# Splitting a kv normalization between VectorE and ScalarE, and moving one weight cast to GpSimd

## The chip, the cores and the metric

The kernel runs on one core of one Trainium2 chip. The metric is the device time of one execution in microseconds (us). Executions were taken in rounds beside executions of the kernel before on the same chip. The granted clock, where it is given, is the share of full speed that the throttle left to the tensor engine (PE) over the whole execution.

## The reference

Linear attention (softmax of q over its last axis, softmax of k over the sequence, no square score matrix), then a two-layer network with a swish gate:

```python
q_s = softmax(q, axis=-1); k_s = softmax(k, axis=2)            # q, k, v: (8, 8, 576, 64)
kv  = np.einsum('bhsd,bhse->bhde', k_s, v)                      # 64 x 64 per batch and head
x   = np.einsum('bhsd,bhde->bhse', q_s, kv)                     # -> (4608, 512)
h   = x @ w_in                                                  # 512 -> 2048
out = (h / (1 + np.exp(-beta * h))) @ w_out                     # 2048 -> 512
```

## The kernel before

The work goes batch by batch; the argument is about the first batch only, before the tensor engine is in full swing. Heads are taken in four pairs, the two heads of a pair on partitions 0 to 63 and 64 to 127. For each pair: kv by 18 small matmuls with a column of sums beside it, its normalization into `kvp`, one matmul that makes x transposed, an eviction of x into `xT`, then the up-projection h. Names in profiles: `kv`, `kvp`, `x`, `xT`, `h`, `th` (tanh), `g`, `acc` (output).

```python
def kvz_norm(b, j, n=1):
    t = att_of.pop((b, j, n))                        # PSUM: 128 x 65, kv and its sum
    rk = work.tile([P, n, 1], F32, tag="rk", bufs=2, ...)
    nc.vector.reciprocal(rk[:], t[:, :, D : D + 1])
    for e in range(2):                               # upper half, lower half
        r = slice(e * D, (e + 1) * D)
        nc.vector.tensor_tensor(
            kvp[r, b, j : j + n, e * D : (e + 1) * D], t[r, :, 0:D], rk[r].to_broadcast((D, n, D)), ALU.mult
        )
...
def xpe(c, j, tag):                                  # x of one pair, in PSUM bank `tag`
    t = x_ps[c, j] = ps.tile([P, MAIN], F32, tag=bank(tag), bufs=1, ...)
    nc.tensor.matmul(t[:], kvp[:, c, j, :], qsT[c][:, :, j, :])
...
def hpe(c, j, kts, tag="h"):                         # unit j of h, slices kts of w_in
    ...
def w_castk(blk, kt, eng):                           # one 128x512 slice of w_in to bf16
    evac(eng, w_in_b[blk][kt][:, 0, :], wst["in", blk][:, kt, :])
```

The order of the first batch, cut to what matters (`A` ScalarE, `V` VectorE, `G` GpSimd):

```python
kvz_mm(0, 2, "acc2", 1)
xpe(0, 0, "b3")
vz_cast(0, 3, A, part=1)
...
kvz_mm(0, 3, "acc3", 1)
xpe(0, 1, "acc0")                 # x of pair 1 sits in bank acc0
w_castk(0, 0, G)
xev(0, 0, A)
kvz_norm(0, 3)
xpe(0, 2, "acc1")
xev(0, 1, A)                      # its eviction, on ScalarE
hpe(0, 0, [0], "b0")
hpe(0, 1, [0], "b1")
xev(0, 2, V)
w_castk(0, 1, A)
xpe(0, 3, "acc2")
w_castk(0, 2, G)
hpe(0, 3, [0], "b2")
xev(0, 3, V)
hpe(0, 2, [0], "acc0")            # unit 2 of h takes over bank acc0
...
hpe(0, 7, [1])
hpe(0, 4, [2])                    # the first matmul on the second half of w_in's block 1
```

The softmax here doesn't subtract the row's maximum and nothing guards it: scores larger than these inputs give would overflow.

Of the kernel before, what the change touches and what calls it, by code (L numbers as in the profile page):

```python
# [12 lines left out]
ACTF = mybir.ActivationFunctionType  # L13
# [4 lines left out]
def kernel(  # L18
# [10 lines left out]
    nc = tc.nc  # L29
    P = nc.NUM_PARTITIONS  # L30
    B, H, S, D = q.shape
# [37 lines left out]
    kvp = const.tile([P, NW, HP, P], BF16, name="kvp")  # L69
# [100 lines left out]
    def evac(eng, dst, src):  # L170
        if eng is nc.scalar:
            eng.copy(dst, src)  # L172
        else:
            eng.tensor_copy(dst, src)  # L174
# [8 lines left out]
    def kz_exp(b, j):  # L183
        if j == 0:
            ek_buf(b)
        nc.scalar.activation(ek[b][:, j, :], k_st[b][:, j, :], ACTF.Exp)  # L186
# [28 lines left out]
    def vz_cast(b, j, eng, m=1, part=None):  # L215
        r = slice(0, RW) if part is None else (slice(0, 5), slice(5, RW))[part]
        evac(
            eng,
            va[b][:, j : j + m, r, 0:D],
            v_st[b][:, j : j + m, :].rearrange("p j (i d) -> p j i d", i=RW)[:, :, r, :],  # L220
        )
# [63 lines left out]
    def bank(tag):  # L285
        if tag not in turns:
            return tag
        turns[tag] += 1
        return (HB if tag == "h" else AB)[(turns[tag] - 1) % 2]
# [17 lines left out]
    def kvz_mm(b, j, tag=None, n=1):  # L307
        if tag is not None:
            t = ps.tile([P, n, D1], F32, tag=bank(tag), bufs=1, name=f"kv{b}_{j}")
            for jl in range(n):  # L310
                att_of[b, j + jl] = t[:, jl : jl + 1, :]
            att_of[b, j, n] = t
        t = att_of[b, j]
        for i in range(RW):
            for e in range(2):
                r = slice(e * D, (e + 1) * D)
                nc.tensor.matmul(  # L317
                    t[r, 0, :],
                    ek[b][r, j, ds(i * D, D)],
                    va[b][r, j, i, :],  # L320
                    start=(i == 0),
                    stop=(i == RW - 1),
                    tile_position=(e * D, e * D),
                )

    def kvz_norm(b, j, n=1):
        t = att_of.pop((b, j, n))
        rk = work.tile([P, n, 1], F32, tag="rk", bufs=2, name=f"rk{b}_{j}")
        nc.vector.reciprocal(rk[:], t[:, :, D : D + 1])
        for e in range(2):  # L330
            r = slice(e * D, (e + 1) * D)
            nc.vector.tensor_tensor(
                kvp[r, b, j : j + n, e * D : (e + 1) * D], t[r, :, 0:D], rk[r].to_broadcast((D, n, D)), ALU.mult
            )
# [52 lines left out]
    def xpe(c, j, tag):  # L387
        t = x_ps[c, j] = ps.tile([P, MAIN], F32, tag=bank(tag), bufs=1, name=f"x{c}_{j}")
        nc.tensor.matmul(t[:], kvp[:, c, j, :], qsT[c][:, :, j, :])  # L389

    def xev(c, j, eng, part=None):
        n = MAIN // 2
        cols = slice(0, MAIN) if part is None else slice(part * n, part * n + n)
        evac(eng, x_of(c)[:, j, cols], x_ps[c, j][:, cols])
# [4 lines left out]
    def hpe(c, j, kts, tag="h"):  # L399
        if (c, j) not in h_of:  # L400
            h_of[c, j] = ps.tile([P, MAIN], F32, tag=bank(tag), bufs=1, name=f"h{c}_{j}")
        h = h_of[c, j]
        for kt in kts:
            nc.tensor.matmul(  # L404
                h[:],
                w_unit(j, kt),
                x_of(c)[:, kt, :],
                start=(kt == 0),
                stop=(kt == KT - 1),
            )  # L410
# [123 lines left out]
    V, A, G = nc.vector, nc.scalar, nc.gpsimd  # L534
# [22 lines left out]
    def w_castk(blk, kt, eng):  # L557
        evac(eng, w_in_b[blk][kt][:, 0, :], wst["in", blk][:, kt, :])
# [89 lines left out]
    q_ev(0, 1, V)  # L648
    q_ev(0, 3, V)
    kz_exp(0, 3)  # L650
    kvz_norm(0, 0)
    kvz_mm(0, 1, "b1", 1)
    vz_cast(0, 2, A, part=1)
    vz_cast(0, 2, G, part=0)
    kvz_norm(0, 1)
    kvz_mm(0, 2, "acc2", 1)
    xpe(0, 0, "b3")
    vz_cast(0, 3, A, part=1)
    vz_cast(0, 3, G, part=0)
    kvz_norm(0, 2)  # L660
    kvz_mm(0, 3, "acc3", 1)
    xpe(0, 1, "acc0")
    w_castk(0, 0, G)
    xev(0, 0, A)
    kvz_norm(0, 3)
    xpe(0, 2, "acc1")
    xev(0, 1, A)
    hpe(0, 0, [0], "b0")
    hpe(0, 1, [0], "b1")
    xev(0, 2, V)  # L670
    w_castk(0, 1, A)
    xpe(0, 3, "acc2")
    w_castk(0, 2, G)
    hpe(0, 3, [0], "b2")
    xev(0, 3, V)
# [247 lines left out]
    for n in range(1, NCH):  # L923
        c = order[n]
        for w in SEQ[max(m for m in SEQ if m <= n)].split():
            kind, j = w[0], int(w[1:].rstrip("a"))
# [63 lines left out]
```

## Time and profile before

| | kernel before |
|---|---|
| time, median of the first 3 runs | 281.63 us (281.60 to 282.54) |
| span of the profiled execution | 279.8 us |
| PE busy | 274.7 us, 98% |
| VectorE, ScalarE, GpSimd busy | 174.9, 162.6, 39.0 us |
| DMA between 14.69 and 19.42 us | 398 GB/s |

In this execution PE stands still for 5.1 us: 2.2 us in the first 20 us, 2.85 us behind its last matmul, and under 0.1 us in all the time between. An edit to the first batch can touch only the first of these.

In what follows I use four marks, read from the start times of single matmuls in the trace's records: the first kv matmul, the 16th matmul of h (the last of the first four units), the *gated matmul* (`hpe(0, 4, [2])`, the first that needs the second half of w_in's block 1), and the first output matmul. "Front" means the time from the first mark to the second.

### The profile page before, as it was taken

Reading aid. Unit: us, or ns where it says so; the run is one execution under the profiler, and the core shown is the slowest. Engines: PE = TensorE matmul, PEld = TensorE weight load, DVE = VectorE, ACT = ScalarE, POOL = GpSimd, SP = SyncE. Lnnn points to the kernel's source line nnn. Section 1 sums busy time; section 2 is a strip of 40 time slices with the busy share of each in tenths; the row PEclk is TensorE's granted clock in tenths of the full one; section 3 lists DMA queues with packets and bytes.
Section 4 is the critical chain, followed back from the end, with each engine's and each line's share of the span. In section 5 each row is a group of like instructions: output and inputs, shape, how many; then the busy total and the mean of one; then the engine's idle time right before and its main releaser. Section 6 shows DMA issues by size and latency. Waiting matters only on the chain.

```text
span 279.8 us, 4474 instructions
## 1 busy us (share of the span) xinstructions
PE 274.7 (98%) x1738; PEld 128.2 (46%) x1738; DVE 174.9 (62%) x285; ACT 162.6 (58%) x248; POOL 39.0 (14%) x59
## 2 busy tenths in 40 slices
PE   8899999999999999999999999999999999999995
PEld 3544454444444444444444444444444544445444
DVE  3964786994478456944595549553864596354362
ACT  3767885947486447744684458444733574454451
POOL 1554237133030003000300030000000000000000
DMA  7999999999972993199319941641144034005004
GB/s 250 389 395 392 386 388 318 331 289 227 270 237 38 253 274 93 64 251 291 96 76 197 305 139 75 134 93 81 69 90 138 0 150 77 0 0 152 0 0 150
DMA packets 55317, 50.09 MB, mean 179 GB/s; under 512 B 26617, under 2 KB 47489, under 8 KB 55297
## 3 DMA queue, kind: packets, MB, share of 16 engines
q1 hardware_dynamic: 54368, 48.97, 59.8%
q10 hardware_dynamic: 928, 0.85, 0.9%
q8 instruction: 13, 0.21, 0.3%
q14 instruction: 8, 0.06, 0.1%
HBM read 36.71 MB, written 9.44 MB: 165 GB/s over the span
## 4 chain that ended last, share of the span: by engine, by line
PE 92%; DMA 6%; SPq 1%; ACT 0%; issue 0%
PE acc L453 44%; PE h L404 43%; DMA w_in<-in_moe_w_in_dram 3%; DMA v_st<-in_v_dram 3%; PE kv L342 2%; PE x L373 1%; PE acc L445 1%; PE kv L317 1%; PE tp L298 0%; PE x L389 0%; ACT w_in_b L172 0%; SPq L578 0%; SPq L132 0%; SPq L109 0%; SPq L135 0%
## 5 line engine op out<-in xcount | busy, mean ns | idle before, releaser
L418 DVE SCALAR_TENSOR_TENSOR g<-th,h 128x512 bf16<-128x512 bf16 x144 | 96.1, 681 | 79.7 <-ACT th L414 79.3
L414 ACT ACTIVATE th<-h,beta_t 128x512 bf16<-128x512 f32 x144 | 97.8, 687 | 81.1 <-PE h L404 80.3
L404 PE MATMUL h<-xT,w_in_b 128*128 128x512 bf16 x576 | 143.3, 379 | 0.1
L453 PE MATMUL acc<-w_out_b,g 128*128 128x512 bf16 x560 | 141.0, 379 | 0.0
L404 PEld LDWEIGHTS <-w_in_b 128*128 128x128 bf16 x576 | 56.0, 98 | 66.4 <-ACT w_in_b L172 0.6
L453 PEld LDWEIGHTS <-g 128*128 128x128 bf16 x560 | 53.8, 98 | 65.9 <-issue 2.5
L174 POOL CAST va<-v_st 128x320 bf16<-128x320 f32 (+2 forms) x14 | 16.6, 1193 | 107.9 <-DMA v_st<-in_v_dram 107.9
L262 DVE TENSOR_REDUCE rq<-eq 128x16 f32<-128x1024 bf16 (+1 forms) x20 | 22.1, 1105 | 5.7 <-ACT eq L251 5.3
L268 DVE TENSOR_TENSOR eq<-eq,rq 128x1024 bf16<-128x1024 bf16 (+1 forms) x19 | 22.1, 1168 | 0.1
L172 ACT CAST xT<-x 128x512 bf16<-128x512 f32 x18 | 9.9, 588 | 16.9 <-PE x L373 14.9
L251 ACT ACTIVATE eq<-q_st 128x1024 bf16<-128x1024 f32 (+1 forms) x18 | 16.9, 955 | 3.5 <-DMA q_st<-in_q_dram 3.5
L174 DVE COPY o<-acc 128x512 f32<-128x512 f32 (+2 forms) x20 | 12.6, 642 | 3.6 <-PE acc L453 3.4
L172 ACT COPY o<-acc 128x512 f32<-128x512 f32 (+1 forms) x18 | 9.5, 571 | 8.6 <-PE acc L453 4.7
L174 DVE CAST xT<-x 128x512 bf16<-128x512 f32 x18 | 11.5, 684 | 2.6 <-PE x L373 1.8
L193 ACT ACTIVATE ek<-k_st 128x1024 bf16<-128x1024 f32 x12 | 12.6, 1051 | 0.0
L532 PE MATMUL warm<-xT 128*128 128x512 bf16 x24 | 7.7, 490 | 1.2 <-DVE xT L613 1.2
L174 POOL CAST w_in_b<-w_in 128x512 bf16<-128x512 f32 (+1 forms) x9 | 5.9, 663 | 6.2 <-DMA w_in<-in_moe_w_in_dram 6.1
L174 POOL CAST w_out_b<-w_out 128x1024 bf16<-128x1024 f32 x5 | 5.2, 1042 | 6.4 <-DMA w_out<-in_moe_w_out_dram 6.4
L186 ACT ACTIVATE ek<-k_st 128x576 bf16<-128x576 f32 x8 | 5.2, 679 | 0.9 <-DMA k_st<-in_k_dram 0.9
L263 DVE RECIPROCAL rq<-rq 128x16 f32<-128x16 f32 (+1 forms) x20 | 4.9, 243 | 0.7
L342 PEld LDWEIGHTS <-ek 128*64 128x64 bf16 x192 | 4.1, 111 | 2.5 <-issue 2.5
L532 PEld LDWEIGHTS <-xT 128*128 128x128 bf16 x24 | 2.8, 121 | 5.2 <-issue 3.0
(49 smaller groups left out, 84.9 us busy)
## 6 DMA issues: line engine op xcount, KB each, us to landing
out_dram<-o SPq DMA_DIRECT2D x14, 512.0 KB, 3.2
q_st<-in_q_dram SPq DMA_DIRECT2D x25, 256.0 KB, 4.1
k_st<-in_k_dram SPq DMA_DIRECT2D x6, 1024.0 KB, 8.7
v_st<-in_v_dram SPq DMA_DIRECT2D x6, 1024.0 KB, 11.3
w_in<-in_moe_w_in_dram SPq DMA_DIRECT2D x6, 512.0 KB, 9.8
v_st<-in_v_dram SPq DMA_DIRECT2D x8, 288.0 KB, 8.0
w_out<-in_moe_w_out_dram SPq DMA_DIRECT2D x4, 512.0 KB, 8.9
w_out<-in_moe_w_out_dram SPq DMA_DIRECT2D x2, 1024.0 KB, 10.4
```

Source lines behind the costliest of these rows:

```text
L172: eng.copy(dst, src)
L174: eng.tensor_copy(dst, src)
L193: nc.scalar.activation(ek[b][:, :, h, :].rearrange("p i h d -> p h i d"), k_st[b][:, h, 0 : R * D].rearrange("p h (i d) -> p h i d", i=R), ...
L251: nc.scalar.activation(eq[b][:, :, s * m : (s + 1) * m, :].rearrange("p i h d -> p h i d"), q_st[b][:, s * m : (s + 1) * m, :].rearrange(" ...
L262: nc.vector.tensor_reduce(rq[b][:, 0, :, h], eq[b][:, :, h, :], axis=AX.X, op=ALU.add)
L268: eng.tensor_tensor(eq[b][:, :, h, :], eq[b][:, :, h, :], rq[b][:, 1, :, h].unsqueeze(3).to_broadcast((P, R, m, D)), ALU.mult,)
L342: nc.tensor.matmul(t[r * D : (r + 1) * D, j, :], ek[b][:, i, hd, :] if i < R else ekt[(b // 2) % 2][:, ds(hd * D, D)], va[b][:, i, hd, :] ...
L404: nc.tensor.matmul(h[:], w_unit(j, kt), x_of(c)[:, kt, :], start=(kt == 0), stop=(kt == KT - 1),)
L414: nc.scalar.activation(th[:], h_of[c, j][:], ACTF.Tanh, scale=beta_t[:, j : j + 1])
L418: nc.vector.scalar_tensor_tensor(out=g[:], in0=th_of.pop((c, j))[:], scalar=1.0, in1=h_of[c, j][:], op0=ALU.add, op1=ALU.mult)
L453: nc.tensor.matmul(acc[st][:], g[:, ds(st * P, P)], w_out_b[:, j, :], start=(j == 0), stop=(j == NJ - 1),)
L532: nc.tensor.matmul(t[:], xT[2][:, 0, 0:P], xT[2][:, 0, :])
```

## The change

The intent: x of pairs 2 and 3 waits for VectorE, so let ScalarE multiply the lower half of pairs 0 and 3 by the same reciprocal (a copy with a per-partition scale). In return ScalarE gives a weight cast to GpSimd, which stood idle there. Pair 0's normalization also moves behind a v cast in the order of recording, so that ScalarE does that cast first.

```diff
-    def kvz_norm(b, j, n=1):
+    def kvz_norm(b, j, n=1, split=False):
...
         for e in range(2):
             r = slice(e * D, (e + 1) * D)
+            if split and e == 1:
+                nc.scalar.activation(kvp[r, b, j, D : 2 * D], t[r, 0, 0:D], ACTF.Copy, scale=rk[r, 0, :])
+                continue
...
-    kvz_norm(0, 0)
     kvz_mm(0, 1, "b1", 1)
     vz_cast(0, 2, A, part=1)
+    kvz_norm(0, 0, split=True)
...
-    kvz_norm(0, 3)
+    kvz_norm(0, 3, split=True)
...
     xev(0, 2, V)
-    w_castk(0, 1, A)
     xpe(0, 3, "acc2")
+    w_castk(0, 1, G)
```

The edit moves the lines behind it by 3 (L404 to L407, the multiply L332 to L335; the scaled copy is L333).

## The prediction

> **What bounds the kernel now.** I read the page first: the tensor engine (PE) is busy 98% of the span, and the chain that ended last is almost nothing but matmuls. So a change off the tensor engine can pay only where the tensor engine stands still.
>
> ```profile
> PE 274.7 (98%) x1738; PEld 128.2 (46%) x1738; DVE 174.9 (62%) x285; ACT 162.6 (58%) x248; POOL 39.0 (14%) x59
> ...
> PE 92%; DMA 6%; SPq 1%; ACT 0%; issue 0%
> ```
>
> Next I read the same chain in order of time, limited to the first 20 us, because all the edited lines run between 11 and 16 us. Columns: start us, length us, what ran.
>
> ```profile
> 2.68 8.01 DMA v_st<-in_v_dram
> 10.70 0.02 issue
> 10.71 8.02 DMA w_in<-in_moe_w_in_dram
> 18.73 0.02 issue
> 18.75 0.63 ACT w_in_b L172
> 19.38 0.05 issue
> 19.43 0.61 PE h L404 x2
> ```
>
> The reader is to see that the chain does not pass through anything that the change edits. It goes through two transfers: a slice of v lands at 10.69 us and lets the queue issue the second half of w_in's second block at 10.71; that lands at 18.73, is cast on ScalarE, and releases a matmul at 19.43. The whole work of the first unit between 11 and 18.7 us is beside the chain. From 19.43 on the chain is matmul after matmul.
>
> Last I read the timeline of the stretch that the change edits (start us, length us, engine, line, operation, count, then the idle time before it and who ended it).
>
> ```profile
> 11.88 0.46 DVE L332 TENSOR_TENSOR kvp<-kv,rk 64x64 bf16<-64x64 f32 x2
> 12.22 0.41 ACT L172 CAST va<-v_st 128x256 bf16<-128x256 f32 x1 [0.24 <-DMA v_st<-in_v_dram]
> 12.37 0.17 DVE L329 RECIPROCAL rk<-kv 128x1 f32<-128x1 f32 x1
> ...
> 13.77 0.10 PEld L389 LDWEIGHTS <-kvp 128*128 128x128 bf16 x1 [0.44 <-DVE kvp L332]
> ...
> 14.15 0.62 ACT L172 CAST w_in_b<-w_in 128x512 bf16<-128x512 f32 x1
> 14.29 1.28 POOL L174 CAST w_in_b<-w_in 128x512 bf16<-128x512 f32 x2 [0.75 <-DMA w_in<-in_moe_w_in_dram]
> 14.46 0.10 PEld L389 LDWEIGHTS <-kvp 128*128 128x128 bf16 x1 [0.36 <-DVE kvp L332]
> ...
> 18.75 0.62 ACT L172 CAST w_in_b<-w_in 128x512 bf16<-128x512 f32 x1 [0.23 <-DMA w_in<-in_moe_w_in_dram]
> ...
> 19.42 1.84 PEld L404 LDWEIGHTS <-w_in_b 128*128 128x128 bf16 x10 [0.58 <-ACT w_in_b L172]
> ```
>
> Here is the author's motive: twice the weight load of an x matmul waits for VectorE's normalization of kv (0.44 and 0.36 us), and GpSimd stands 0.75 us idle in front of 14.29. Here is also what will swallow the gain: the weight load at 19.42 waited for the cast of 18.75, and ScalarE itself had sat 0.23 us waiting for the transfer.
>
> **What the Trainium skill says.** "ScalarE: Activation LUTs", section "What ACT_TABLE_LOAD costs", gives an ACTIVATE as 186 ns + 0.833 ns per element, about 93 ns more for each per-partition pointer operand, with some 93 ns of overlap between neighbours. The trace roughly agrees: the 128x512 cast out of PSUM takes 586 ns (page: 612), the 128x512 tanh with beta as a pointer scale 687 ns (page: 706). The same page, "Table sets: the hidden batching unit", says that cheap functions such as copy are in every set, so the scaled copy should load no table; the comparison of the instruction streams shows one table load before and one after. "Perfetto Trace Analysis", "Roofline", puts the ceiling of a core's 16 DMA engines at about 435 GB/s; between 14.69 and 19.42 us this trace moves 398 GB/s with a DMA share of 1.04, so transfers there are bound by bandwidth. "TensorE: Matmul & The Clock Gate", "Step-by-step: what each phase is for", gives 216 ns between back-to-back 512-column matmuls; the trace has four in 0.86 us.
>
> **The change part by part.**
> VectorE loses two 64x64 multiplies of 222 ns (lower half of pairs 0 and 3); the reciprocals and pairs 1 and 2 stay. ScalarE gains two 64x64 scaled copies. Estimate for one: the 128x16 copy took 153 ns, the 128x512 one 586, so 64 columns are 153 + 48 x 0.87 = 195, plus 101 for the pointer scale (687 - 586): 0.30 us. ScalarE loses one 0.62 us cast, which becomes one 0.61 us cast on GpSimd. ScalarE is then about even.
>
> Pair 0. Reciprocal ends 11.85 and ScalarE is free at 11.98, so its copy runs from about 12.0 to 12.3. The upper half on VectorE ends 12.10. x's first weight load came at 12.51, in the tensor engine's order behind pair 2's kv matmuls, so it does not move. ScalarE's cast of v slips from 12.22 to about 12.28 and ends about 12.68, still before GpSimd's part of it (12.25 + 0.46 = 12.71): kv of pair 3 still starts at 12.83.
>
> Pairs 1 and 2. VectorE is free at 12.10 and not 12.34, but pair 1's matmuls started at 11.71, and pair 0's needed 11.69 - 11.10 = 0.59 us to the reciprocal: pair 1 is ready at 12.30, not before. It starts there and not at 12.37, so I gain only **0.07 us** of the 0.24 freed. Pair 2 moves with it: the weight load of 13.77 goes to 13.70. Its reciprocal now also waits for ScalarE's copy of pair 0 (two buffers of rk), long done.
>
> Pair 3. Reciprocal 13.68 to 13.85, upper half to 14.10 on VectorE, ScalarE's copy 13.9 to 14.2. x of pair 3 then no longer waits for it but for its turn: 13.70 + 3 x 0.216 = 14.35, against 14.46. Gain at this place **0.11 us**. The price is that ScalarE's eviction of x 1 slips from 13.67 to about 14.1, ending 14.7. Its first reader comes three matmuls after 14.35, at about 15.0: free.
>
> The cast of the second w_in slice. Slices land about 0.68 us apart (12.90, then 14.27 two slices later), so this one at about 13.6; GpSimd casts it from 13.6 to 14.2, in its gap, ready earlier than 14.77, and the next cast still starts at 14.29. Nothing waits for it before 15.0. The SP queue's wait for the four casts that free this staging buffer was set by the last GpSimd cast (15.57) and stays so.
>
> Sum: the tensor engine enters the stretch at 14.69 about 0.1 us earlier. It had 20 matmuls from 14.69, and the last ended its issue at about 19.17, a hole of 0.26 us before 19.43. After the change the hole is about 0.36 us, because 18.73 + cast + 0.05 is unmoved. **Net: 0.0 us.** What follows 19.43 was dense and has the same order.
>
> **The rivals.**
> (1) The front gain survives: if the transfer were not what ends the hole, I would gain 0.1 us, at most the 0.3 us that removing both waits wholly would give (281.3). For it: the two waits are real. Against it: ScalarE idles for the transfer before 18.75, and GpSimd waits for the same transfer 1.19 us.
> (2) A new wait takes the place: a scaled copy much slower than 0.30 us on ScalarE's queue ahead of the v cast and x's eviction. To cost anything it must push the tensor engine past the 0.36 us hole, so each copy would have to take some 0.7 us. A table load is excluded by the instruction streams. Then +0.1 to +0.5 us.
> (3) GpSimd becomes late: its cast of 0.61 us could stretch as the v cast at 10.00 did (1.05 us beside VectorE's bf16 multiply, 0.67 for the next of the same size). Then the third and fourth slices come 0.4 us late, at about 16.0, where the matmul on the fourth stands at about 15.9: 0.1 us, again inside the hole.
> (4) Execution-to-execution scatter: one of three runs before was 282.54, 0.9 above the others. This is larger than any effect above.
>
> **Range and chances.** Prediction 281.6 us. Below: the full front gain of 0.3 gives 281.3, so 281.25. Above: a slow copy or a median caught by the scatter of +0.9, so 282.05. Two per cent is 5.6 us; the whole edited stretch is 8 us long, so neither side is credible: faster 0.005, same 0.985, slower 0.01.
>
> **What would show it.** In the changed profile: the transfer still ends about 18.7 us, followed by ScalarE's cast and matmuls at about 19.4; the hole's wait at 19.42 grows from 0.58 to about 0.7; ScalarE's wait for the transfer grows from 0.23 to about 0.3; the wait of x's weight load for pair 3 vanishes or shrinks, that of pair 2 stays near 0.4; the copies take about 0.3 us; the span stays 279.8 within 0.2. I am wrong if the chain of waits leaves the transfer at 10.71 to 18.73, or if the span moves although it doesn't.

## The result and the profile after

| | before | changed |
|---|---|---|
| median of 6 runs, us | 281.64 | 281.81 |
| all runs, us | 281.54 to 282.97 | 281.52 to 281.96, and one of 411.51 |

The ratio of the fast runs is 0.9992, with a 95% interval of 0.9969 to 1.0014: no difference. (A ratio is the mean time of the fast runs of the kernel named over that of the kernel before in the same rounds, so it is not quite the ratio of the medians above; the median of the five fast runs is 281.79.) In microseconds the interval reaches from 0.9 less to 0.4 more. So the times alone can't show a shift of 0.2 us either way, and what follows about such shifts is read from profiles. The run of 411.51 us is the profiled one. Its granted clock is 0.657; the row of the PE clock shows it, in tenths for 40 slices of the span:

```profile
PEclk8666666666666666666666666666666666666666
```

PE ran at six tenths of its speed from the second slice on. That is a state of that one execution: five other executions of the same program kept a clock of 0.999 or 1.0. I compare nothing with it, and took the profile again (the first experiment). The following lines are that second profile of the changed kernel: first its chain of waits up to 22 us (start, length, what).

```profile
2.25 7.77 DMA v_st<-in_v_dram
10.02 0.05 issue
10.07 1.66 POOL va L174 x2
11.73 0.04 issue
11.77 0.87 PE kv L317 x36
...
14.09 0.45 PE h L407 x2
14.53 0.58 ACT xT L172
15.11 0.04 issue
15.16 6.58 PE h L407 x29
```

The reader is to see that the second transfer (w_in, 10.71 to 18.73) has gone from the chain. It now runs through the front itself: the landing of v, GpSimd's cast, kv, x, and then, new, an eviction of x on ScalarE. (The step from h to this eviction is not to be trusted: the eviction reads x of pair 1, which PE had finished before, and the timeline below has it right behind ScalarE's copy, 14.19 + 0.31 = 14.50.) So the time is the same, but not for the reason that I gave. The timeline of the same execution shows what became of the waits (last bracket: the idle time before, and who ended it).

```profile
12.26 0.31 ACT L333 ACTIVATE kvp<-kv,rk 64x64 bf16<-64x64 f32 x1 [0.20 <-PE kv L317]
...
13.67 0.17 DVE L329 RECIPROCAL rk<-kv 128x1 f32<-128x1 f32 x1
13.69 0.10 PEld L392 LDWEIGHTS <-kvp 128*128 128x128 bf16 x1 [0.25 <-DVE kvp L335]
...
13.88 0.22 DVE L335 TENSOR_TENSOR kvp<-kv,rk 64x64 bf16<-64x64 f32 x1
...
14.19 0.31 ACT L333 ACTIVATE kvp<-kv,rk 64x64 bf16<-64x64 f32 x1 [0.55 <-DVE kvp L335]
14.52 0.58 ACT L172 CAST xT<-x 128x512 bf16<-128x512 f32 x1
14.55 0.10 PEld L392 LDWEIGHTS <-kvp 128*128 128x128 bf16 x1 [0.52 <-ACT kvp L333]
...
15.16 4.42 PE L407 MATMUL h<-xT,w_in_b 128*128 128x512 bf16 x19 [0.22 <-ACT xT L172]
...
18.67 0.61 POOL L174 CAST w_in_b<-w_in 128x512 bf16<-128x512 f32 x1 [0.70 <-DMA w_in<-in_moe_w_in_dram]
...
19.32 0.10 PEld L407 LDWEIGHTS <-w_in_b 128*128 128x128 bf16 x1 [0.24 <-ACT w_in_b L172]
```

Three things are read here. The wait of pair 2's x fell from 0.44 to 0.25 us: the gain that was intended. The copy of pair 3 did not start when the reciprocal was done (13.84) but at 14.19, just after VectorE's multiply (13.88 + 0.22 = 14.10): the two halves ran one after the other, and x of pair 3 waited 0.52 us for the copy. And behind that copy ScalarE evicted x of pair 1 only at 14.52, for which PE waited 0.22 us at 15.16. (One record of h just before it is missing from this trace. By the start times, at 0.216 us a matmul, it came 0.18 us late, which is all that the front became longer.) The first line shows the same of pair 0: its copy started at 12.26, also 0.1 us behind VectorE's multiply (11.94 + 0.22 = 12.16), although the bracket names kv.

### The profile page after: what moved, and what is told of

It reads as the page before. It is cut to its first block, busy times and chain, and to the rows that moved or that the text cites. A ratio compares the mean times of both kernels' runs of the same rounds, so it can differ in the third digit from the quotient of the medians.

```text
span 409.7 us, 4476 instructions
## 1 busy us (share of the span) xinstructions
PE 405.1 (99%) x1738; PEld 157.8 (39%) x1738; DVE 179.3 (44%) x283; ACT 164.7 (40%) x249; POOL 39.6 (10%) x60
## 4 chain that ended last, share of the span: by engine, by line
PE 96%; DMA 2%; POOL 0%; SPq 0%; ACT 0%; issue 0%; DVE 0%; ACTq 0%
PE h L407 46%; PE acc L456 45%; DMA v_st<-in_v_dram 2%; PE kv L345 1%; PE acc L448 1%; PE x L376 1%; PE kv L317 1%; PE x L392 1%; POOL va L174 0%; PE tp L298 0%; SPq L581 0%; SPq L132 0%; SPq L109 0%; ACT kvp L333 0%; PE x L367 0%
## 5 line engine op out<-in xcount | busy, mean ns | idle before, releaser
L407 PE MATMUL h<-xT,w_in_b 128*128 128x512 bf16 x576 | 209.0, 513 | 0.0
L456 PE MATMUL acc<-w_out_b,g 128*128 128x512 bf16 x560 | 205.4, 511 | 0.0
L421 DVE SCALAR_TENSOR_TENSOR g<-th,h 128x512 bf16<-128x512 bf16 x144 | 98.4, 686 | 181.8 <-ACT th L417 181.8
L407 PEld LDWEIGHTS <-w_in_b 128*128 128x128 bf16 x576 | 70.2, 122 | 113.7 <-issue 112.7
L456 PEld LDWEIGHTS <-g 128*128 128x128 bf16 x560 | 66.2, 120 | 113.9 <-issue 110.6
L535 PE MATMUL warm<-xT 128*128 128x512 bf16 x24 | 9.0, 550 | 1.2 <-DVE xT L616 1.2
L448 PE MATMUL acc<-w_out_b,g 128*128 128x128 bf16 (+1 forms) x48 | 6.9, 298 | 0.0
L357 DVE RECIPROCAL rk<-kv 128x4 f32<-128x4 f32 x6 | 1.1, 182 | 12.3 <-PE kv L345 12.3
L345 PEld LDWEIGHTS <-ek 128*64 128x64 bf16 x192 | 5.0, 127 | 3.8 <-issue 3.8
L448 PEld LDWEIGHTS <-g 128*128 128x128 bf16 x48 | 4.7, 117 | 4.2 <-issue 3.8
```

What stands on the lines that cost most here:

```text
L345: nc.tensor.matmul(t[r * D : (r + 1) * D, j, :], ek[b][:, i, hd, :] if i < R else ekt[(b // 2) % 2][:, ds(hd * D, D)], va[b][:, i, hd, :] ...
L407: nc.tensor.matmul(h[:], w_unit(j, kt), x_of(c)[:, kt, :], start=(kt == 0), stop=(kt == KT - 1),)
L421: nc.vector.scalar_tensor_tensor(out=g[:], in0=th_of.pop((c, j))[:], scalar=1.0, in1=h_of[c, j][:], op0=ALU.add, op1=ALU.mult)
L448: nc.tensor.matmul(acc[st][:, 0:hw], g[:, ds((R - 1) * P, P)], w_out_b[:, j, ds(lo, hw)], start=(j == 0), stop=(j == NJ - 1),)
L456: nc.tensor.matmul(acc[st][:], g[:, ds(st * P, P)], w_out_b[:, j, :], start=(j == 0), stop=(j == NJ - 1),)
```

## The experiments

My theory after the result: the copy waits for VectorE's multiply of the same PSUM tile; this makes the front longer, not shorter; the loss is hidden because the kernel before had a hole in front of the gated matmul, made by the w_in transfer. The rival from the prediction: the front gained 0.1 us and the transfer swallowed it.

The marks of the first profile and of the ten experiments whose front ran at full clock (us; "front" as defined above; "gap" is the time from the matmul ahead of the gated one to the gated one, 0.21 when PE does not wait; in some traces one record of h is missing, which was allowed for):

| run | first kv | front | gap | first output | span minus first output |
|---|---|---|---|---|---|
| before, first profile | 11.10 | 6.40 | 0.47 | 21.60 | 258.25 |
| e12 before again | 11.12 | 6.41 | 0.69 | 21.85 | 258.24 |
| e1 changed again | 11.16 | 6.58 | 0.21 | 21.57 | 258.26 |
| e2 split only | 10.91 | 7.03 | 0.21 | 21.77 | 258.25 |
| e4 before, transfer in two | 11.33 | 6.40 | 0.21 | 21.57 | 258.30 |
| e5 changed, transfer in two | 11.29 | 6.59 | 0.21 | 21.71 | 258.30 |
| e6 before, dose | 11.15 | 6.90 | 0.21 | 21.89 | 258.24 |
| e7 changed, dose | 11.30 | 7.08 | 0.22 | 22.72 | 258.24 |
| e8 ScalarE first | 11.19 | 6.61 | 0.21 | 21.64 | 258.25 |
| e9 pair 0 only, transfer in two | 11.13 | 6.81 | 0.21 | 21.79 | 258.30 |
| e11 pair 0 only | 11.39 | 6.26 | 0.22 | 22.09 | 258.26 |

(e3 and e10, cast only, ran at a reduced clock in the front and are told of below.) The last column is the finding that makes the rest readable: from the first output matmul to the end, every one of these takes 258.24 to 258.30 us. The span of a profiled execution is when that matmul starts, plus a constant. Each front stands for one execution, but where the order of work is the same and no slice landed late it repeats within 0.01 us: 6.40, 6.41 and 6.40 in the kernel before, 6.58 and 6.59 in the changed one.

**e1: the changed kernel again** (no edit).

> The changed kernel once more, because its profile fell into an execution at a granted clock of 0.657. Theory (a transfer of w_in, landing at about 18.7 us, sets when the tensor engine gets going for good): fast executions within 0.3 us of before, the transfer still lands near 18.73, the tensor engine's hole before the gated matmul grows from 0.26 to about 0.36 us, the scaled copies take about 0.30 us. Rival (the front gain survives): span 0.1 to 0.3 us shorter.

Measured: 281.71 us median (281.53 to 282.99), ratio 0.9996 (0.9975 to 1.0017). The copies take 0.31 us, near the 0.30 expected. GpSimd's cast of the last slice starts on its landing at 18.67. But the hole before the gated matmul did not grow: it is gone, and the front grew from 6.40 to 6.58 us. Both theories of that expectation were wrong in this point: there was no front gain to swallow or to keep.

**e2: the split only.**

```diff
+    w_castk(0, 1, A)
     xpe(0, 3, "acc2")
-    w_castk(0, 1, G)
```

> Only the scaled copies go to ScalarE; the cast of the second w_in slice stays on ScalarE, behind x 1's eviction. Theory: that cast ends about 0.45 us later than before (near 15.2 instead of 14.77) and its first reader, due at about 15.0, waits 0.2 to 0.3 us; this is inside the hole of 0.36, so the time stays within 0.3 us of before. Rival (no transfer gate): about 0.2 us slower than the whole change.

Measured: 281.80 us, one run. The cast stands behind the late eviction of x 1 and ends at 15.50. The front is 7.03 us, 0.45 longer than with the whole change. So moving the cast to GpSimd is what keeps the split affordable. The time is within the scatter, as expected, because v happened to land early in this execution (first kv at 10.91).

**e3 and e10: the cast only.**

```diff
     xev(0, 2, V)
-    w_castk(0, 1, A)
     xpe(0, 3, "acc2")
+    w_castk(0, 1, G)
```

> Only the cast of the second w_in slice goes to GpSimd; kv is normalized on VectorE as before. Theory: the waits of x's weight loads stay at 0.44 and 0.36 us, GpSimd casts the slice from about 13.6 to 14.2 and is not late for the third, the time stays within 0.3 us of before. Rival (GpSimd late): the casts of the third and fourth slice end 0.4 us or more later.

> The cast-only kernel once more, because its first look had the tensor engine at a granted clock of 0.57 between 12 and 16 us. Theory (the cast costs and gains nothing, the copy of pair 3 makes the front longer): x of pair 2 and 3 as in the kernel before (2.68 and 3.36 us after the first kv matmul), no wait for a bank behind x 3, matmul after matmul up to the gate, then a hole of 0.1 to 0.3 us. Rival (the cast on GpSimd makes the front longer): a hole ahead of the matmuls on the third or fourth slice.

Measured: 282.48 and 282.31 us, one run each. Both are inconclusive, since PE's clock was halved for 3.4 us in the very stretch that matters (0.50 from 12.31 to 15.72 us in e3, from 11.97 to 15.38 in e10; the 0.58 below is the mean of a longer stretch). Here is the second one by stretches of 4 us (length; busy us of PE, weight loads, VectorE, ScalarE, GpSimd; then PE's clock, DMA share, GB/s):

```profile
8.00:12.00 4.00, 3.13 (x54) 1.94 (x53) 3.79 (x11) 3.08 (x7) 2.99 (x4) 1.00 1.05 385
12.00:16.00 4.00, 4.00 (x54) 2.17 (x48) 2.92 (x13) 1.58 (x3) 2.93 (x6) 0.58 1.07 398
16.00:20.00 4.00, 4.00 (x20) 1.68 (x18) 2.18 (x4) 2.31 (x5) 1.78 (x3) 1.00 1.02 394
```

Matmuls that start 0.22 us apart elsewhere start 0.43 apart here. What both do show: GpSimd took the four casts back to back in 2.63 and 2.66 us and was late for none, as the theory had it. Such executions, with a mean clock of 0.994, also occur with the kernel before (four of those in the rounds, at 282.52 to 282.62 us) and with the changed one (282.69 and 282.99). They make part of the upper group of the scatter. Whether the cast-only kernel is more prone to it, as two of two might suggest, stays open.

**e5 and e4: the gating transfer in two**, in the changed kernel and in the kernel before.

```diff
-    w_load("in", 1, 1)
+    for kt in (2, 3):
+        nc.sync.dma_start(wst["in", 1][:, kt, :], w_in_d[:, kt, ds(512, 512)])
```

> The changed kernel with the gating 512 KB transfer of w_in issued as two of 256 KB. Theory: the first half lands about 0.65 us earlier (near 18.1) and the gated matmul no longer waits for it; the second half lands near 18.73 and is needed two matmuls later. The hole of about 0.36 us closes and the time falls by 0.2 to 0.36 us against the changed kernel. Rival (the front, not the transfer, sets the end): no gain, and the hole that opens is before x's matmuls alone.

> The kernel before, with the gating 512 KB transfer of w_in issued as two of 256 KB. Theory (in the kernel before the transfer makes a hole of 0.26 us that the front does not need): the first half lands near 18.1 us, ScalarE casts it right after its third tanh, the gated matmul follows the one ahead of it at the usual 0.22 us pitch, and the time falls by about 0.25 us. Rival (the front sets the end in both kernels): no gain, as the same edit gave none in the changed kernel.

Measured: e5 281.76 us median (281.49 to 281.96), ratio 0.9982 (0.9968 to 0.9996), but the kernel before had three executions with a mean clock of 0.994 in these rounds and three more above 282.1 us, and e1 in the same rounds has 281.71: no gain over the changed kernel. The trace says why: there was no hole left to close, ScalarE goes from its third tanh straight to the cast. e4 has 281.65 us median (281.61 to 281.92) against 281.67, ratio 1.0 (0.9988 to 1.0012). In its trace the hole is gone and the gated matmul follows at 0.21 us, as the theory said: 8.07 us after the first kv matmul, where the kernel before needed 8.33. Yet the time did not fall. Two reasons are seen: v landed later in this execution (first kv at 11.33, against 11.10), and the part after the first output matmul is 0.05 us longer in all three kernels with the transfer in two. The edit itself can't have made v late: its two transfers are issued at 10.94 and 11.70 us, when the first two slices of v had landed (10.18 and 10.92). The first is large enough to hide 0.25 us in a profile; that it should do so in the median of five runs was not expected, and I can't say that it did. The gain of 0.25 us is not shown in the time, nor ruled out: the interval of e4's ratio is 0.34 us wide to either side.

**e8: ScalarE's half recorded first.**

```diff
-        for e in range(2):
+        for e in (1, 0) if split else (0, 1):
```

> The changed kernel with ScalarE's copy recorded ahead of VectorE's multiply of the same pair. Theory (the two read one PSUM tile and are put in order of recording, whichever it is): the copy now starts some 0.06 us after the reciprocal, VectorE's multiply waits for it, x of pair 3 is no earlier than in the changed kernel (about 14.5), but x 1's eviction starts 0.2 us or more earlier and the wait of the matmul that takes x 1's bank shrinks from 0.22 us to nothing. Rival (the copy waits for something else): the copy still starts 0.35 us after the reciprocal's end.

Measured: 281.66 us, one run. The timeline around pair 3:

```profile
13.96 0.17 DVE L329 RECIPROCAL rk<-kv 128x1 f32<-128x1 f32 x1
...
14.16 0.31 ACT L333 ACTIVATE kvp<-kv,rk 64x64 bf16<-64x64 f32 x1 [0.42 <-DVE rk L329]
...
14.49 0.59 ACT L172 CAST xT<-x 128x512 bf16<-128x512 f32 x1
14.50 0.22 DVE L335 TENSOR_TENSOR kvp<-kv,rk 64x64 bf16<-64x64 f32 x1 [0.38 <-ACT kvp L333]
...
14.77 0.10 PEld L392 LDWEIGHTS <-kvp 128*128 128x128 bf16 x1 [0.46 <-DVE kvp L335]
```

The order is turned over: the copy starts 0.03 us after the reciprocal's end, and now VectorE's multiply waits 0.38 us for it. So the two engines take turns in the order of recording, and the split gives no overlap either way. The bank wait disappeared, as expected, but x of pair 3 came later (3.58 us after the first kv, against 3.39 in e1), since pair 0's multiply had waited too; the front is 6.61 us, no better. I had put x 1's eviction 0.2 us earlier; it came 0.06 earlier against the first kv matmul.

What the wait is for can be read from the built instruction streams. In the changed kernel the copy of pair 3 waits for the 26th increment of VectorE's semaphore; the reciprocal gives the 25th, the multiply the 26th. In a build (not run) whose copy reads another tile in place of kv, it waits for the 25th; with another destination, or with a constant scale, it still waits for the 26th. So it is the shared PSUM source. The Trainium skill, "PSUM — Partial Sum Buffer", section "PSUM bank collisions raise a hardware error", says that two engines may not be at the same bank and 32-partition quadrant at once, readers included, while different quadrants of one bank are fine. The halves here are partitions 0 to 63 and 64 to 127, different quadrants, so by that page the wait is stricter than it has to be. No run here takes it away, so this is argued, not shown.

**e6 and e7: a dose of delay.** VectorE's first multiply of pair 2 is done three times.

```diff
-        for e in range(2):
+        for e in [0] * again + [0, 1]:
...
-    kvz_norm(0, 2)
+    kvz_norm(0, 2, again=2)
```

> The kernel before with VectorE's first multiply of pair 2 done three times, so 0.44 us more ahead of x of pair 2. Theory (0.26 us of slack before the gated matmul): matmuls up to the gate come 0.44 us later, those after it only about 0.18 us. Rival (no slack): all 0.44 us later, also after the gate.

> The changed kernel with VectorE's first multiply of pair 2 done three times (0.50 us in the kernel before). Theory (the change has used up the slack that the kernel before has): counted from the first kv matmul to the first output matmul, 10.41 us become about 10.9, all of the 0.50; in the kernel before the same dose made 10.50 to 10.74. Rival (both have the same slack): about 10.65.

Measured: e6 282.24 us, e7 282.97 us, one run each. In the kernel before, the dose made the front 0.50 us longer (6.90 against 6.40), but the first output matmul came only 0.29 us later than in the first profile of that kernel and 0.04 later than in the second. The hole took the rest: it was 0.26 us in the one (0.47 - 0.21) and 0.48 in the other. In e7 the front became 0.50 us longer (7.08 against 6.58), and the first output matmul came 1.15 us later than in e1. That is more than all of the dose, so the run agrees that no slack is left, but it does not measure it: 0.14 us of it are a later first kv matmul, and two further waits are for slices of w_in that landed late in this execution, as the timeline shows.

```profile
18.24 1.79 POOL L174 CAST w_in_b<-w_in 128x512 bf16<-128x512 f32 x3 [2.34 <-DMA w_in<-in_moe_w_in_dram]
...
18.91 0.10 PEld L407 LDWEIGHTS <-w_in_b 128*128 128x128 bf16 x1 [0.63 <-POOL w_in_b L174]
...
19.46 0.12 PEld L407 LDWEIGHTS <-w_in_b 128*128 128x128 bf16 x2 [0.46 <-POOL w_in_b L174]
```

The first half of block 1, which landed at about 16.4 in the kernel before, landed at 18.2 here.

**e11 and e9: pair 0 only**, without and with the transfer in two (the edit of e4).

```diff
-    kvz_norm(0, 3, split=True)
+    kvz_norm(0, 3)
```

> The changed kernel with pair 3 back on VectorE: pair 0 split, the cast on GpSimd, the transfers as before. Theory: x of pair 2 about 0.07 us earlier than in the kernel before, x 3 too, no bank wait, so the front is the shortest of all (about 8.0 us from the first kv matmul to the end of the seventh unit's second matmul); the transfer then sets the end and the time stays within 0.2 us of before. Rival (the split of pair 0 costs too): the front as long as in the changed kernel.

> The changed kernel with pair 3 back on VectorE (pair 0 alone split, cast on GpSimd) and the gating transfer in two. Theory: without the copy of pair 3 on ScalarE, x 1 is evicted as early as before and the front gains the 0.07 to 0.1 us of pair 0; with the transfer out of the way, the gain and the hole are both kept: 0.3 us less than before. Rival (moving pair 0 costs as pair 3 did): no better than the kernel before with the transfer in two.

Measured: e11 282.01 us median (281.62 to 283.18) against 281.69, ratio 1.0014 (0.9995 to 1.0032); e9 282.06 us (281.46 to 282.44) against 281.67, ratio 1.001 (0.9998 to 1.0022). In e11 the front is the shortest of all, 6.26 us: 0.14 less than in the kernel before and 0.32 less than with both pairs split. This is the cleanest statement on the change: splitting pair 0 and moving the cast gain 0.14 us, splitting pair 3 loses 0.32. Without the copy of pair 3, x 1's eviction starts 2.64 us after the first kv matmul, where e1 had 3.36, and no matmul waits for its bank:

```profile
14.03 0.59 ACT L172 CAST xT<-x 128x512 bf16<-128x512 f32 x1 [0.17 <-PE x L392]
...
14.62 0.10 PEld L392 LDWEIGHTS <-kvp 128*128 128x128 bf16 x1 [0.36 <-DVE kvp L335]
```

Of the two, it is the split of pair 0 that brings the 0.14 us, as far as x of pair 2 tells: it came 2.54 us after the first kv matmul here, in e1, and in e2 too, where the cast was not moved, against 2.68 before.

The time did not follow. In e11's profiled execution the first half of block 1 landed at 17.6 and PE waited for it twice, ahead of the gate; in e9's a slice of v and one of w_in's first block came late, and its front was 6.81. Neither version beats the kernel before, and both medians lean towards slower without being clear of it. Why transfers, issued in the same order, land up to 2.1 us apart between executions is open.

**e12: the kernel before again** (no edit).

> The kernel before, unchanged, for a second profile. Theory: the front takes the same 8.07 us from the first kv matmul to the seventh unit's third, but for the transfer; the hole that the transfer makes is between 0.1 and 0.4 us, depending on how the landings of v and of w_in fall. Rival (the hole was peculiar to one execution): none.

Measured: 281.87 us, one run. The chain of waits:

```profile
2.67 8.09 DMA v_st<-in_v_dram
10.76 0.02 issue
10.78 8.21 DMA w_in<-in_moe_w_in_dram
18.98 0.02 issue
19.00 0.63 ACT w_in_b L172
19.63 0.05 issue
19.68 0.39 PE h L404
```

It is the same chain as in the first profile; the transfer landed 0.25 us later, the gated matmul started 0.25 us later (19.68 against 19.43), and so did the first output matmul. In the kernel before, this transfer does set the time, and it moves by as much as the change was worth.

## Why the prediction was right or wrong

**The time, the range and the class: right.** 281.81 us against 281.6, inside 281.25 to 282.05, and no difference beyond the scatter. But the number came by luck as much as by reasoning: of the two parts that I set against each other, a front gain of 0.1 us and a hole to swallow it, the first had the wrong sign, and either sign would have left the time within the scatter.

**What bounds the kernel before: right.** Both of its profiles have the transfer of w_in in the chain and a hole in front of the gated matmul, of 0.26 and 0.48 us.

**The size of the copy, the absence of a table load, the cast in GpSimd's gap: right.** The copies took 0.31 us (0.30 expected), and GpSimd served all slices; the next wait on it was for a landing.

**Pair 0 and its gain for pair 2: right in direction, too small in size.** I gave 0.07 us; x of pair 2 came 2.54 us after the first kv matmul, where it had been 2.68: 0.14. Pair 1's reciprocal started 1.13 us after the first kv matmul, against 1.27 before. I had put its earliest start at 1.20 (12.30 - 11.10), by borrowing the 0.59 us that pair 0 took from its first matmul to its reciprocal; that was too long. What I had at no cost was not quite free: pair 0's copy ran behind VectorE's half as pair 3's did, at 12.26 and not at 12.0, and so x of pair 0, which needs both halves, came 1.46 us after the first kv matmul, where it had been 1.42; kv of pair 3 and x of pair 1 behind it came as much later.

**Pair 3: wrong, and this is the step that failed.** The prediction has "ScalarE's copy 13.9 to 14.2", beside VectorE's half. It started after VectorE's half, at 14.19, because both read one PSUM tile and are recorded in that order. I had seen in the comparison of the streams that the copy waits for VectorE, and took that for the reciprocal without counting which instruction it was. x of pair 3 gained nothing (3.39 us after the first kv, against 3.37).

**The eviction of x 1 "free": wrong.** I looked for the first matmul that reads xT of pair 1 and missed that unit 2 of h takes over bank acc0, in which that x lies. It comes two matmuls after x of pair 3, and waited 0.22 us by the trace, 0.18 by the start times. The reader that I had looked at comes one matmul later, due at 15.20 by the same pitch, and would not have waited, since the eviction ended at 15.10.

**The hole "about 0.36 us": wrong in sign.** The front became 0.18 us longer (6.58 against 6.40), not 0.1 shorter, so the hole shrank, in e1 to nothing. The front alone does not close it: in e1 the first kv matmul was also 0.06 us later and the transfer landed 0.11 earlier (GpSimd's cast on it began at 18.67, and at 18.78 before). The wait of the weight load at the gate, which I had growing from 0.58 to 0.7 us, became 0.24. By my own test ("I am wrong if the chain of waits leaves the transfer") the mechanism was wrong, although its upshot, that some tenths in the front vanish in that hole, holds in the profiles: it swallowed a loss where I had it swallow a gain.

**Scatter larger than the effect: right.** It showed as differing landings, as a clock halved for 3.4 us of the front, and once as a clock of 0.657 for a whole execution. What causes each is not settled here.

## What to carry to other kernels

When work on one PSUM tile is split between two engines, check which instruction the second one's wait names: if it is the first engine's half and not the common input, the halves run in turn, and the longer queue is all that is bought. When a matmul is late, look for who still holds its output bank as well as for who makes its inputs. And before valuing tenths of a microsecond ahead of a transfer's landing, take the profile twice: here the landing moved by 0.25 us between two executions of the same program.

## What the Trainium skill lacked or had wrong

- "PSUM — Partial Sum Buffer" states the rule by bank and quadrant. It doesn't warn that the layer that records a kernel may put two readers of one tile in order even where their partitions lie in different quadrants. Here that made the copy of pair 3 start 0.35 us after its reciprocal's end (13.84 to 14.19).
- "TensorE: Matmul & The Clock Gate" tells of a half-rate clock at the start, after idling, and where PE idles briefly again and again. It doesn't tell what makes one execution of a program fall into it and not another. Here e10 had a clock of 0.50 from 11.97 to 15.38 us and matmuls 0.43 us apart, with PE busy for 3.13 us of 8 to 12 us; the kernel before kept 1.00 with PE busy for 3.23 us of the same stretch. Executions with this mean clock (0.994) took 282.31 to 282.99 us, against about 281.7.
- No page that I used says how far landings scatter between executions when the DMA engines are saturated (a share of 1.04 here). The same 512 KB transfer landed at 18.73 and 18.98 us in two executions of one program, and the half ahead of it between 16.1 and 18.2 us over the kernels tried.
